# Bucket equality on VectorE instead of sign products on TensorE, for one of eight head groups

## The chip, the cores and the metric

The kernel runs on one core of a Trainium2 chip. The core has a matrix engine (TensorE, PE in the profile; its weight loads are PEld), a vector engine (VectorE, DVE), an activation engine (ScalarE, ACT), a general-purpose one (GpSimd, POOL) and a queue engine (SyncE, SP) that issues most transfers. Each engine takes its instructions in program order and waits on semaphores. The metric is the device time of one execution in microseconds; lower is better.

## The reference

The computation is hash-bucketed attention for 4 batches of 8 heads (sequence 768, head size 64), followed by a channel block with a residual:

```python
q_bits = (np.einsum('bhsd,dk->bhsk', q, proj) > 0)      # 6 bits, k likewise
q_bucket = np.sum(q_bits * powers, axis=-1)             # 0..63
mask = q_bucket[:, :, :, None] == k_bucket[:, :, None, :]
scores = np.where(mask, 0.125 * q @ k.T, -1e9)
attn = softmax(scores) ; x = attn @ v                   # heads side by side: 512 wide
xn = (x - mean) / sqrt(var + 1e-6) * g
out = x + relu(xn @ w_ch1) @ w_ch2                      # 512 -> 2048 -> 512
```

A query sees only keys whose six projection signs are the same as its own.

## The kernel before

**Tiles.** The work is cut into 12 units u (4 batches of 3 query blocks of 256), each unit into 2 head groups g of 4 heads, each group into 3 key pairs kp of 2 x 128 keys. That gives 72 steps, s = 6u + 3g + kp. A step has three parts:

- `S_` (TensorE, line 516): the scores of 4 heads x 256 keys x 256 queries, transposed, into two PSUM tiles (scA, scB). For every 128 keys there are three passes over the 4 heads; each head uses its own 32 rows of the matrix engine, so four matmuls of a pass run side by side. The first pass (`rep == 0`) multiplies the sign rows: `G` holds for every query and key the six signs as +0.5 or -0.5, so the product is 1.5 where all signs agree and at most 1.0 otherwise. The other two passes add q.k, in two halves of 32. q was scaled by 2^-11 before, so that the sign product stands far above it.
- `E_` (ScalarE, line 522): the exponential of 2 heads at a time, with a scale of 256 and a bias that takes the full sign product off again. Where a sign differs, the exponent is lower by 128 or more, and the result is zero. The result is the bf16 tile E, of which there are four buffers.
- `A_` (TensorE, line 541): E as weights times v with a column of ones, 32 matmuls of 65 columns, summed over the three key pairs in one PSUM tile (acc).

After the last key pair of a group, VectorE divides by the sum of the weights (`na`, `nb`), takes statistics (`nc`), and, when both groups are done, centres and scales by g (`ce`). The tile is transposed by a DMA (`fl`). Then `F_` (TensorE, line 598) makes 256 of the 2048 hidden columns at a time, `R_` (relu, line 606 on ScalarE or 608 on VectorE) brings them to SBUF, `D_` (line 614) does a quarter of the second product for one row tile, `Z_` (line 622) adds the residual, `O_` writes the rows out. F has one PSUM bank, so an F waits for the relu of the F before it; D has another.

**Signs.** For batches 1 to 3, `hm` (line 471) multiplies the transposed q and k by the projection into a PSUM tile `hp`: 128 partitions are 4 chunks of the sequence x 4 heads x 8 bit places, 192 columns each for q and k. `bt` (VectorE, line 480) turns it into +-0.5 in bf16, `mw` (line 489) writes that to DRAM and four `mr` (line 492) read it back in the layout that G needs, one head each.

**Order.** Nothing is scheduled at run time. `ORDER` is a list of words such as `S.t.58.2` or `R.v.7.1` (operation, engine, arguments), issued in turn; it fixes the order on every engine's queue and which engine does each relu, copy and cast. `SLOTS` fixes which buffer each tile of a pool takes. In the list, TensorE's score steps, AV steps, F and D alternate, so that ScalarE and VectorE have time between them. The last batch is u = 9, 10, 11 (steps 54 to 71), its second head group the steps 57 to 59, 63 to 65 and 69 to 71.

Of the kernel before, what the change touches and what calls it, by code (L numbers as in the profile page):

```python
# [8 lines left out]
F32 = mybir.dt.float32  # L9
# [5 lines left out]

ROT = (0, 1, 2)
# [3 lines left out]
mem.v lp.a lx.a.0.1.0.1 tab.a pf.v lx.s.0.0.0.1 warm.t wm.t.0 wm.t.1 wm.t.2 wm.t.3 sel.p  # L20
tn.v.0.0.0 p32.p tn.v.0.1.0 ca.p.0.1.0 lx.s.0.1.1.3 ha.t.0.0.0 wm.t.4 lx.s.1.1.0.3 lx.s.1.0.0.1 ha.t.0.1.0 lv.s.0.0.4 ca.a.0.0.0
lx.s.0.0.1.3 bh.v.0.0.0 wm.t.5 tn.v.0.1.1 ha.t.0.1.1 lw2.p.1 bh.v.0.1.0 ca.p.0.1.1 S.t.0.2 lv.s.0.4.4 E.a.0.0 E.a.0.1
tn.v.0.1.2 tn.v.1.1.1 ca.p.1.1.1 lx.s.1.0.1.3 wm.t.6 wm.t.7 bh.v.0.1.1 ha.t.1.1.1 on.p.0 bh.v.1.1.1 tn.v.1.1.0 S.t.1.2
E.a.1.0 ca.v.0.1.2 gx.p.1.0.0 ha.t.0.1.2 bh.v.0.1.2 E.a.1.1 tn.v.1.0.0 ca.p.1.0.0 ca.v.1.1.0 ha.t.1.1.0 bh.v.1.1.0 tn.v.1.1.2
S.t.2.2 E.a.2.0 cv.p.0.0.0 ha.t.1.0.0 bh.v.1.0.0 S.t.4.2 cv.p.0.0.2 tn.v.0.0.1 hc.t.0.0.1 ca.p.0.0.1 lw1.p.3 bc.v.0.0.1
gx.p.1.0.1 ha.t.1.1.2 LX.s.1.0.0 tn.v.0.0.2 E.a.2.1 E.a.4.0 LX.s.1.0.1 E.a.4.1 bh.v.1.1.2 sl.t.0.0.1 bi.v.0.0.1 cv.p.0.4.2
A.t.0.2 S.t.3.2 A.t.1.2 ca.v.1.1.2 lg.s lw1.p.1 sq.t.0.0 E.a.3.0 A.t.2.2 sc.v.0.0 E.a.3.1 S.t.5.2
E.a.5.0 cv.p.0.4.0 sq.t.0.4 na.v.0.0 nb.v.0.0 lw1.p.2 lw1.p.0 nc.v.0.0 E.a.5.1 S.t.8.2 sc.a.0.4 A.t.5.2
E.a.8.0 E.a.8.1 tu.v.1.0.0.2 lw2.p.0 tn.v.1.0.1 A.t.4.2 ca.p.1.0.1 hc.t.0.0.2 tn.v.1.0.2 A.t.3.2 tu.v.1.0.1.0 bc.v.0.0.2
lw2.p.3 gx.p.1.1.1 tu.v.1.0.0.1 sl.t.0.0.2 na.v.0.1 bi.a.0.0.2 S.t.6.2 E.a.6.0 LX.s.1.1.1 E.a.6.1 hc.t.1.0.1 nb.v.0.1  # L30
hc.t.1.0.2 bc.v.1.0.2 sl.t.1.0.2 bi.a.1.0.2 bc.v.1.0.1 pmem.p S.t.7.2 A.t.8.2 E.a.7.0 lv.s.1.4.1 nc.v.0.1 ce.v.0.1
ce.v.0.0 ft.t.0.1 lv.s.1.4.2 E.a.7.1 fc.a.0.1 sl.t.1.0.1 tu.v.1.0.1.1 bi.v.1.0.1 A.t.6.2 ft.t.0.0 S.t.9.2 E.a.9.0
on.p.1 lw2.p.2 fc.v.0.0 E.a.9.1 F.t.0.6 F.t.0.7 tu.v.1.0.1.2 R.a.0.6 A.t.7.2 tu.v.1.0.0.0 S.t.10.2 R.v.0.7
na.v.1.0 nb.v.1.0 lv.s.1.4.0 tu.v.1.0.0.3 tu.v.1.0.1.3 E.a.10.0 CA.p.1.0.1 F.t.0.3 F.t.0.4 E.a.10.1 A.t.9.2 ca.a.0.0.2
R.v.0.4 ca.a.1.0.2 S.t.11.2 gx.p.1.1.0 LX.s.1.1.0 E.a.11.0 E.a.11.1 lv.s.1.0.0 hm.t.1.0 R.v.0.3 F.t.0.5 S.t.14.2
R.a.0.5 A.t.11.2 A.t.10.2 E.a.14.0 E.a.14.1 bt.v.1.0 na.v.1.1 nb.v.1.1 F.t.0.2 R.a.0.2 S.t.12.2 nc.v.1.0
E.a.12.1 E.a.12.0 lv.s.1.0.1 F.t.0.0 R.v.0.0 mw.s.1.0 F.t.0.1 R.a.0.1 CA.p.1.0.0 tu.v.1.1.1.0 A.t.14.2 nc.v.1.1
ce.v.1.0 S.t.13.2 E.a.13.0 D.t.0.0.0 lv.s.1.0.3 tu.v.1.1.1.2 lv.s.1.4.3 D.t.0.0.1 fl.s.1.0 tu.v.1.1.0.2 ce.v.1.1 fl.s.1.1
tu.v.1.1.0.0 A.t.12.2 E.a.13.1 LX.s.2.0.0 S.t.16.2 E.a.16.0 E.a.16.1 A.t.13.2 tu.v.1.1.1.3 tu.v.1.1.0.1 tu.v.1.1.0.3 rs.p.0
D.t.0.0.2 D.t.0.0.3 mr.s.1.0.1 cv.p.1.4.0 Z.v.0.0 tu.v.1.1.1.1 CA.p.1.1.1 cv.p.1.4.2 S.t.15.2 lv.s.1.0.2 cv.p.1.0.0 E.a.15.0  # L40
mr.s.1.0.2 mr.s.1.0.3 hm.t.1.1 E.a.15.1 D.t.0.1.0 CA.a.1.1.0 S.t.17.2 E.a.17.1 mr.s.1.0.0 bt.v.1.1 mw.s.1.1 mr.s.1.1.3
na.v.2.0 nb.v.2.0 F.t.1.2 R.v.1.2 su.p.1.0 A.t.15.2 E.a.17.0 cv.p.1.0.2 A.t.16.2 F.t.1.6 S.t.18.2 R.a.1.6
nc.v.2.0 F.t.1.5 R.v.1.5 D.t.0.1.1 mr.s.1.1.2 E.a.18.0 A.t.17.2 E.a.18.1 sp.t.1.0 sc.v.1.0 na.v.2.1 S.t.20.2
E.a.20.0 mr.s.1.1.0 lv.s.2.4.1 F.t.1.0 tu.v.2.0.0.0 R.v.1.0 D.t.0.1.2 F.t.1.4 nb.v.2.1 nc.v.2.1 E.a.20.1 tu.v.2.0.0.3
R.a.1.4 S.t.19.2 E.a.19.0 E.a.19.1 D.t.0.1.3 ce.v.2.0 F.t.1.1 LX.s.2.0.1 su.p.1.4 rs.p.1 R.a.1.1 mr.s.1.1.1
Z.v.0.1 lv.s.2.0.1 lv.s.2.4.3 O.s.0.1 tu.v.2.0.1.2 lv.s.2.0.2 A.t.20.2 tu.v.2.0.1.1 S.t.21.2 ce.v.2.1 E.a.21.0 fl.s.2.0
F.t.1.3 D.t.1.0.0 E.a.21.1 A.t.18.2 rs.p.2 S.t.22.2 R.v.1.3 tu.v.2.0.0.1 tu.v.2.0.0.2 CA.v.2.0.0 A.t.19.2 fl.s.2.1
F.t.1.7 na.v.3.0 tu.v.2.0.1.3 O.s.0.2 R.v.1.7 E.a.22.0 E.a.22.1 D.t.1.0.1 S.t.23.2 F.t.2.1 lv.s.2.4.0 D.t.1.0.2
R.v.2.1 LX.s.3.1.0 nb.v.3.0 E.a.23.0 A.t.22.2 E.a.23.1 lv.s.2.0.0 F.t.2.0 LX.s.2.1.1 D.t.1.0.3 R.a.2.0 tu.v.2.0.1.0
CA.p.2.0.1 hm.t.2.0 S.t.24.2 E.a.24.1 Z.v.1.0 nc.v.3.0 bt.v.2.0 mw.s.2.0 sp.t.1.4 sc.v.1.4 A.t.21.2 lv.s.2.0.3  # L50
mr.s.2.0.2 D.t.1.1.0 A.t.23.2 O.s.0.0 E.a.24.0 na.v.3.1 O.s.0.3 tu.v.2.1.1.0 F.t.2.3 mr.s.2.0.3 cv.p.2.0.0 tu.v.2.1.1.1
R.a.2.3 nb.v.3.1 S.t.26.2 LX.s.2.1.0 D.t.1.1.1 E.a.26.0 E.a.26.1 nc.v.3.1 F.t.2.2 R.v.2.2 ce.v.3.1 D.t.1.1.2
mr.s.2.0.1 S.t.25.2 ce.v.3.0 F.t.2.4 LX.s.3.0.1 A.t.24.2 E.a.25.0 D.t.1.1.3 cv.p.2.0.2 R.v.2.4 S.t.29.2 E.a.25.1
tu.v.2.1.1.2 fl.s.3.1 Z.v.1.1 E.a.29.0 A.t.25.2 E.a.29.1 D.t.2.0.0 fl.s.3.0 F.t.2.7 R.a.2.7 S.t.28.2 A.t.26.2
tu.v.2.1.0.3 F.t.2.5 D.t.2.0.1 E.a.28.0 R.v.2.5 tu.v.2.1.0.1 E.a.28.1 na.v.4.0 S.t.31.2 E.a.31.1 tu.v.2.1.1.3 F.t.3.6
R.v.3.6 A.t.29.2 D.t.2.0.2 tu.v.2.1.0.2 tu.v.2.1.0.0 CA.v.2.1.0 E.a.31.0 F.t.2.6 R.a.2.6 O.s.1.3 S.t.27.2 E.a.27.0
D.t.2.0.3 nb.v.4.0 LX.s.3.0.0 O.s.1.2 hm.t.2.1 LX.s.3.1.1 nc.v.4.0 bt.v.2.1 mw.s.2.1 mr.s.2.1.3 Z.v.2.0 tu.v.3.0.0.2
E.a.27.1 tu.v.3.0.0.1 S.t.30.2 E.a.30.0 rs.p.3 su.p.2.0 F.t.3.4 A.t.27.2 R.a.3.4 on.p.2 D.t.2.1.0 D.t.2.1.1
E.a.30.1 F.t.3.1 R.v.3.1 S.t.32.2 CA.a.2.1.1 O.s.1.1 E.a.32.0 D.t.2.1.2 lv.s.3.0.0 F.t.3.2 tu.v.3.0.1.0 R.v.3.2
O.s.1.0 A.t.28.2 E.a.32.1 lv.s.2.4.2 S.t.35.2 E.a.35.0 E.a.35.1 na.v.4.1 F.t.3.0 cv.p.2.4.0 mr.s.2.0.0 D.t.2.1.3  # L60
Z.v.2.1 O.s.2.0 A.t.30.2 R.a.3.0 O.s.2.1 S.t.34.2 lv.s.3.0.2 mr.s.2.1.2 F.t.3.3 A.t.31.2 E.a.34.0 nb.v.4.1
R.v.3.3 tu.v.3.0.1.1 nc.v.4.1 ce.v.4.1 D.t.3.0.0 fl.s.4.1 ce.v.4.0 fl.s.4.0 E.a.34.1 tu.v.3.0.1.2 S.t.33.2 rs.p.4
D.t.3.0.1 A.t.32.2 E.a.33.0 tu.v.3.0.0.3 E.a.33.1 F.t.3.5 R.a.3.5 S.t.37.2 E.a.37.1 tu.v.3.0.0.0 cv.p.2.4.2 na.v.5.0
nb.v.5.0 D.t.3.0.2 A.t.33.2 F.t.3.7 A.t.35.2 E.a.37.0 R.v.3.7 nc.v.5.0 S.t.38.2 E.a.38.0 D.t.3.0.3 Z.v.3.0
mr.s.2.1.1 F.t.4.3 A.t.34.2 O.s.2.2 na.v.5.1 E.a.38.1 R.a.4.3 lv.s.3.0.3 O.s.2.3 tu.v.3.0.1.3 S.t.36.2 E.a.36.1
CA.v.3.0.1 F.t.4.0 R.a.4.0 nb.v.5.1 mr.s.2.1.0 CA.v.3.0.0 D.t.3.1.0 hm.t.3.0 bt.v.3.0 E.a.36.0 S.t.39.2 mw.s.3.0
E.a.39.0 F.t.4.2 A.t.38.2 R.a.4.2 tu.v.3.1.1.3 E.a.39.1 A.t.37.2 F.t.4.5 R.a.4.5 S.t.40.2 sp.t.2.0 sc.v.2.0
# [613 lines left out]
```

## Time and profile before

| | |
|---|---|
| runs | 304.79, 305.19 and 303.57 us; median 304.79 |
| profiled execution | 303.7 us; its span 302.0 us, granted TensorE clock 1.0 throughout |
| TensorE busy | 290.5 us (96%) |
| ScalarE busy | 189.0 us (63%) |
| VectorE busy | 175.9 us (58%) |
| GpSimd busy | 76.4 us (25%) |
| 144 exponentials | 153.5 us, 1111 ns each |
| relus | 49 on VectorE (690 ns), 47 on ScalarE (596 ns) |

How to read it: the span is what the profiler saw of one execution, from the first to the last instruction; busy times are unions of an engine's instructions. Matmuls overlap in the matrix engine, so a bar of a matmul is longer than the time that it adds; what a block adds is read from the start of one block to the start of the next. A row of a group gives line, engine, operation, tiles, shapes, count, then busy time and mean duration of one, then the engine's idle time before them and who ended it.

### The profile page before, as it was taken

The page shows a single profiled execution, that of the slowest core. Times are in us where ns is not written, and L with a number is a line of the kernel's source. Part 1 is how long each engine was busy: PE and PEld are TensorE (multiplying, and loading weights), DVE is VectorE, ACT ScalarE, POOL GpSimd, SP SyncE. Part 2 cuts the span into 40 slices and gives each one's busy share as a digit, 9 for nine tenths or more (in the row PEclk, how much of TensorE's full clock was granted, in tenths as well). Part 3 has the DMA queues.
Part 4 walks back from the last instruction along what each step waited for, and adds up shares of the span by engine and source line. Part 5 has one row for each costly group of instructions (what it writes and reads, how often), then busy time and mean ns, then how long its engine had stood idle before and what let it go on. Part 6 is the DMA issues. An engine that isn't in the chain of part 4 may idle for free.

```text
span 302.0 us, 9823 instructions
## 1 busy us (share of the span) xinstructions
PE 290.5 (96%) x4345; PEld 202.5 (67%) x4394; DVE 175.9 (58%) x364; ACT 189.0 (63%) x206; POOL 76.4 (25%) x103
## 2 busy tenths in 40 slices
PE   8988899999999999999999999999999999999995
PEld 4666677676766767677666776667666776676663
DVE  4878758759767564875749466274554346443322
ACT  2587888778646777777667866854565665643010
POOL 5497062476017101300750002700101001001000
PEclk9999999999999999999999999999999999999999
DMA  6999999718768453420322242012201501003132
GB/s 221 310 299 247 282 212 270 177 35 230 201 159 246 84 217 95 98 72 18 80 66 41 68 100 51 21 35 54 54 2 35 106 2 37 20 2 89 52 87 71
DMA packets 31194, 34.32 MB, mean 114 GB/s; under 512 B 15536, under 2 KB 27824, under 8 KB 31152
## 3 DMA queue, kind: packets, MB, share of 16 engines
q1 hardware_dynamic: 26080, 28.98, 35.0%
q0 software_dynamic: 4224, 4.19, 8.5%
q8 instruction: 34, 0.56, 0.8%
q10 hardware_dynamic: 848, 0.53, 0.7%
q14 instruction: 8, 0.07, 0.1%
HBM read 28.12 MB, written 6.88 MB: 116 GB/s over the span
## 4 chain that ended last, share of the span: by engine, by line
PE 94%; ACT 3%; issue 1%; DVE 0%
PE f L598 29%; PE sc L516 19%; PE acc L541 12%; PE hp L471 3%; ACT E L522 3%; PE hf L359 2%; PE warm L328 1%; PE f_110None L614 1%; PE f_101None L614 1%; PE f L614 1%; PE f_90None L614 1%; PE f_20None L614 1%; PE f_80None L614 1%; PE f_21None L614 1%; PE f_00None L614 1%
## 5 line engine op out<-in xcount | busy, mean ns | idle before, releaser
L522 ACT ACTIVATE E<-sc,bias_sb 128x1024 bf16<-128x1024 f32 x144 | 153.5, 1111 | 60.6 <-PE sc L516 60.6
L598 PE MATMUL f<-xnT,w_sb 128*128 128x256 bf16 x768 | 99.3, 273 | 0.1
L598 PEld LDWEIGHTS <-w_sb 128*128 128x128 bf16 x768 | 70.8, 98 | 22.6 <-issue 7.4
L608 DVE TENSOR_SCALAR hb<-f 128x512 bf16<-128x512 f32 x49 | 33.7, 690 | 59.2 <-PE f L598 58.8
L614 PEld LDWEIGHTS <-hb 128*128 128x128 bf16 x400 | 36.0, 98 | 31.2 <-issue 3.0
L516 PE MATMUL sc<-qb,kb 32*128 32x256 bf16 x1152 | 52.4, 267 | 0.0
L606 ACT ACTIVATE hb<-f 128x512 bf16<-128x512 f32 x47 | 28.0, 596 | 35.9 <-PE f L598 35.9
L541 PEld LDWEIGHTS <-E 128*128 128x128 bf16 x1152 | 42.7, 98 | 8.2 <-issue 3.2
L541 PE MATMUL acc<-vaug,E 128*128 128x65 bf16 x1152 | 46.2, 194 | 0.1
L516 PE MATMUL sc<-G 6*128 6x256 bf16 (+1 forms) x576 | 42.6, 273 | 2.7 <-ACT E L522 2.0
L576 POOL TENSOR_SCALAR rs<-mv 128x2 f32<-128x2 f32 x12 | 7.7, 640 | 106.9 <-DVE mv L570 106.6
L516 PEld LDWEIGHTS <-kb 32*128 32x128 bf16 x1152 | 30.4, 93 | 1.5
L516 PEld LDWEIGHTS <-G 6*128 6x128 bf16 (+1 forms) x576 | 15.7, 91 | 20.7 <-issue 17.4
L417 POOL CAST vaug<-vn 128x768 bf16<-128x768 f32 x16 | 14.0, 884 | 58.3 <-DMA vn<-in_v_dram 44.2
L270 DVE STREAM_TRANSPOSE T<-X 128x384 f32<-128x384 f32 (+2 forms) x52 | 26.8, 542 | 1.2 <-DMA X<-in_k_dram 1.2
L554 DVE SCALAR_TENSOR_TENSOR y<-vsB,acc 128x520 f32<-128x520 f32 x24 | 16.5, 688 | 10.5 <-PE acc L541 10.2
L571 DVE SCALAR_TENSOR_TENSOR xc<-x,mv,gB 128x512 bf16<-128x512 f32 x24 | 18.6, 775 | 0.9
L567 DVE BATCH_NORM_STATS2 st<-x 128x6 f32<-128x256 f32 x48 | 17.7, 412 | 0.3
L563 DVE TENSOR_TENSOR x<-y,rc 128x512 f32<-128x512 f32 x24 | 16.8, 699 | 0.8
L425 POOL TENSOR_TENSOR t<-vn 128x768 f32<-128x768 f32 x6 | 10.9, 1812 | 0.0
L281 POOL CAST kb<-T 128x1536 bf16<-128x1536 f32 x3 | 4.4, 1461 | 22.3 <-DVE T L270 22.3
L270 DVE STREAM_TRANSPOSE tp<-X 128x256 f32<-128x256 f32 x24 | 9.0, 416 | 1.4 <-DMA X<-in_q_dram 0.9
(113 smaller groups left out, 236.7 us busy)
## 6 DMA issues: line engine op xcount, KB each, us to landing
out_dram<-x SPq DMA_DIRECT2D x45, 128.0 KB, 2.0
X<-in_k_dram SPq DMA_DIRECT2D x7, 768.0 KB, 5.8
X<-in_q_dram SPq DMA_DIRECT2D x6, 768.0 KB, 4.7
vn<-in_v_dram SPq DMA_DIRECT2D x24, 192.0 KB, 6.0
w_sb<-in_moe_w_ch_dram POOLq DMA_DIRECT2D x8, 512.0 KB, 15.9
vn<-in_v_dram SPq DMA_DIRECT2D x2, 768.0 KB
X<-in_q_dram SPq DMA_DIRECT2D x2, 512.0 KB, 12.2
Bd<-B SPq DMA_DIRECT2D x6, 96.0 KB, 2.5
```

The costliest lines, as they stand in the source:

```text
L270: nc.vector.transpose(d[:, j], s[:, j, kj0 : kj0 + n])
L516: nc.tensor.matmul(sc(s, i // 2)[:, i % 2, 256 * kk : 256 * kk + 256], lh, rh, start=(rep == 0), stop=(rep == 2), skip_group_check=True,)
L522: nc.scalar.activation(E(s)[:, heads(h)], sc(s, h), AF.Exp, scale=EXP_SCALE, bias=bias_sb)
L541: nc.tensor.matmul(acc[:, qt, (D + 1) * i : (D + 1) * (i + 1)], E(s)[:, i, 256 * kk + P * qt : 256 * kk + P * qt + P], vaug(u // 3)[:, 4 * ...
L554: nc.vector.scalar_tensor_tensor(yt(u, g), vs, EPS_ROW, made[f"acc{u}{g}"][:, :, :A], op0=AOP.mult, op1=AOP.add,)
L563: nc.vector.tensor_tensor(xo, a[:, :, :, 0:D], rc.to_broadcast([P, 2, 4, D]), op=AOP.mult)
L567: nc.vector.bn_stats(stats(u)[:, qt, g], xt(u)[:, qt, 256 * g : 256 * g + 256])
L571: nc.vector.scalar_tensor_tensor(xc(u)[:, t], xt(u)[:, t], mv(u)[:, t, 0:1], gB, op0=AOP.subtract, op1=AOP.mult,)
L598: nc.tensor.matmul(f1[:, n].rearrange("p (t x) -> p t x", t=2), w1_sb[:, dt, P * nt : P * nt + P], xnT(u)[:, :, dt], start=(dt == 0), stop ...
L606: nc.scalar.activation(hb(u)[:, 2 * p : 2 * p + 2], f1, AF.Relu)
L608: eng.tensor_scalar_max(hb(u)[:, 2 * p : 2 * p + 2], f1, 0.0)
L614: nc.tensor.matmul(f2, hb(u)[:, nt, P * t : P * t + P], w2_sb[:, nt, half(h)], start=(nt == 0), stop=(nt == NNT - 1),)
```

## The change

For the second head group of the last batch (`COMPARED = ((3, 1),)`) the kernel no longer puts the signs into the scores. Its nine score steps leave the first pass out; the exponential is taken without the bias; and VectorE multiplies the exponentials, in place, by whether the bucket numbers of query and key are equal (`K_`), before A uses them. The bucket numbers are made by seven small matmuls of the +-0.5 signs with powers of two (`nu`): the queries' into 16 partitions, the keys' with the key on the partition, which is how E lies. `ne` copies both out of PSUM; `nw` writes the queries' numbers to DRAM and `nr` reads them back, spread to all 128 partitions (`QB`, 6 KB each), in a buffer of the X pool. The five transfers `mw` and `mr` of this group go. POOL makes the powers of two (`pl`).

`K_` is 4 operations per half step (2 heads x 2 key blocks), 72 in all.

The list ORDER is new as a whole. Up to about u = 4 TensorE's, ScalarE's and VectorE's queues are as before but for single words; behind it F, D, R, A and S stand in another order, 44 relus are on VectorE and 52 on ScalarE, one cast of k or q (`CA.3.1.0`) and two small copies (`sc.3.0`, `sc.3.4`) are on VectorE instead of ScalarE, loads of v stand earlier on SyncE, and at the end part of the last row tile's D stands ahead of the other's.

```diff
+COMPARED = ((3, 1),)
...
+    def pl(eng):
+        nc.gpsimd.memset(zero, 0.0)
+        nc.gpsimd.memset(places, 0.0)
+        for n in range(NB):
+            nc.gpsimd.affine_select(
+                out=places, in_=places, pattern=[[-8, 16]], base=-n, channel_multiplier=1, compare_op=AOP.not_equal, fill=2.0**n,
+            )
...
+    def QB(b, g):
+        return sb(f"QB{b}{g}", [P, 4, S], BF16, "X", 4)
+
+    def nu(eng, b, g):
+        hp = made[f"hp{b}{g}"]
+        nc.tensor.matmul(hp[:16, :W], places, Bt(b, g)[:, 0], start=True, stop=True, skip_group_check=True)
+        kn = hp[:, 384:408].rearrange("p (a k i) -> p a k i", a=2, k=3)
+        for w in range(3):
+            for par in range(2):
+                lo = 64 * ((par + w) % 2)
+                nc.tensor.matmul(
+                    kn[lo : lo + 64, :, (3 * par + w) // 2], Bt(b, g)[:, 1, 64 * w : 64 * w + 64],
+                    places.rearrange("p (a r i) -> p r a i", a=2, r=2)[:, par], start=True, stop=True, skip_group_check=True,
+                )
+
+    def ne(eng, b, g):
+        hp = made[f"hp{b}{g}"]
+        nc.vector.tensor_copy(Qn(b, g), hp[:16, :W])
+        nc.vector.tensor_copy(Kn(b, g).rearrange("p k i -> p (k i)"), hp[:, 384:408])
+
+    def nw(eng, b, g):
+        eng.dma_start(out=Qd(b, g).rearrange("i c w -> c i w"), in_=Qn(b, g))
+
+    def nr(eng, b, g):
+        eng.dma_start(out=QB(b, g).rearrange("p i s -> p (i s)"), in_=Qd(b, g).rearrange("i c w -> (i c w)").partition_broadcast(P))
+
+    def K_(eng, s, h):
+        u, g, kp = s // 6, (s % 6) // 3, s % 3
+        b, q0 = u // 3, 256 * (u % 3)
+        for i in range(4)[heads(h)]:
+            for kk in range(2):
+                e = E(s)[:, i, 256 * kk : 256 * kk + 256]
+                eng.scalar_tensor_tensor(
+                    e, QB(b, g)[:, i, q0 : q0 + 256], Kn(b, g)[:, 2 * kp + kk, i : i + 1], e, op0=AOP.is_equal, op1=AOP.mult,
+                )
...
     def S_(eng, s, h):
...
+            first = 1 if (b, g) in COMPARED else 0
-            for rep in range(3):
+            for rep in range(first, 3):
...
     def E_(eng, s, h):
-        nc.scalar.activation(E(s)[:, heads(h)], sc(s, h), AF.Exp, scale=EXP_SCALE, bias=bias_sb)
+        bias = zero if (s // 18, (s % 6) // 3) in COMPARED else bias_sb
+        nc.scalar.activation(E(s)[:, heads(h)], sc(s, h), AF.Exp, scale=EXP_SCALE, bias=bias)
```

The part of the new list in which the compared steps of u = 9 stand, cut to TensorE's and VectorE's words:

```
S.t.58.2 F.t.6.4 D.t.6.0.0 D.t.6.0.1 R.v.6.4 F.t.7.1 K.v.58.1 R.v.7.1 S.t.57.2 D.t.6.0.2 F.t.7.7 R.v.7.7 A.t.56.2
D.t.6.0.3 Z.v.6.0 K.v.57.0 F.t.7.2 S.t.59.2 D.t.6.1.0 K.v.58.0 F.t.7.0 R.v.7.0 na.v.9.0 D.t.6.1.1 S.t.60.2 F.t.7.3
D.t.6.1.2 D.t.6.1.3 K.v.59.0 F.t.7.5 ce.v.8.0 A.t.58.2 S.t.61.2 K.v.59.1 F.t.7.4 K.v.57.1 A.t.57.2 A.t.59.2 nb.v.9.0
R.v.7.4 F.t.7.6
```

and those around the last ones:

```
S.t.70.2 Z.v.8.1 A.t.66.2 K.v.70.0 K.v.71.0 F.t.10.6 na.v.11.0 D.t.9.0.0 D.t.9.0.1 F.t.10.7 D.t.9.0.2 F.t.10.3 D.t.9.0.3
K.v.69.0 A.t.69.2 F.t.10.1 K.v.70.1 A.t.70.2 nb.v.11.0 Z.v.9.0 A.t.71.2
```

The last D words are, before: `D.11.0.3`, then `D.11.1.0.0 D.11.1.1.0 D.11.1.2.0 D.11.1.3.0` (384 columns) and `D.11.1.0.1` to `D.11.1.3.1` (128 columns); after, `D.11.0.3` is followed only by `D.11.1.3.0` and the last three of 128 columns.

## The prediction

> **What bounds the kernel now.** I read the page's first part, then the windows, then the chain that ended last, and only then the rows of the operations that the change touches.
>
> ```profile
> PE 290.5 (96%) x4345; PEld 202.5 (67%) x4394; DVE 175.9 (58%) x364; ACT 189.0 (63%) x206; POOL 76.4 (25%) x103
> PE 94%; ACT 3%; issue 1%; DVE 0%
> ```
>
> TensorE is busy for 96% of the span and carries 94% of the chain. The windows show where it isn't busy:
>
> ```profile
> 80.00:277.00 197.00, 194.21 (x2927) 135.82 (x2959) 111.74 (x217) 128.39 (x140) 35.24 (x43) 1.00 0.29 74
> 200.00:270.00 70.00, 69.10 (x971) 48.74 (x984) 33.75 (x64) 40.33 (x46) 4.45 (x6) 1.00 0.16 34
> ```
>
> The columns are stretch, length, and busy time of PE, PEld, DVE, ACT, POOL, then the granted clock. In the long middle TensorE misses 2.8 of 197 us, so no new order of the work can win more than that there. From 200 to 270, where S.58 to A.69 of the last batch lie, VectorE works 33.8 of 70 us: 36 us are free, and the change wants most of them.
>
> The chain gives the prices of TensorE's blocks:
>
> ```profile
> 233.28 0.77 PE sc L516 x22
> 234.05 0.98 PE f L598 x8
> 235.03 0.98 PE acc L541 x32
> 236.01 0.87 PE f L598 x8
> ```
>
> A score step S is 0.77 us, and the block behind it is 0.11 longer (0.98 against 0.87), so S counts 0.88. F is 0.87, one AV step A is half of 0.98 = 0.49, a D quarter about 0.87 (1.73 for eight matmuls).
>
> **What the change takes from TensorE.** One score step in detail:
>
> ```profile
> 63.21 0.29 PE L516 MATMUL sc<-G 6*128 6x256 bf16 x4
> 63.33 0.39 PE L516 MATMUL sc<-qb,kb 32*128 32x256 bf16 x8
> 63.55 0.28 PE L516 MATMUL sc<-G 6*128 6x256 bf16 x4
> 63.66 0.39 PE L516 MATMUL sc<-qb,kb 32*128 32x256 bf16 x8
> ```
>
> From the start of a G pass to the next pass are 0.12 and 0.11 us (the bars overlap, since four row groups run together). Nine steps lose both passes: 9 x 0.23 = 2.07 us off the path. Bounds: nothing, if the rest of the step doesn't close up, to a third of 0.88, 9 x 0.29 = 2.6. I take 2.07, the row itself.
>
> **What it adds to TensorE.** nu is one matmul of 192 columns and six of 8 columns. The nearest small ones are the four 64-column matmuls of L383, between 0.11 and 0.21 us start to start (28.37 to 28.58 is the longer). Seven such are 0.2 to 0.37; hm, with 32 matmuls, takes 1.44. I take 0.35. Its wait for bt (0.56 on VectorE) has a score step of 0.77 before it, and F.6.7, which waits for ne (two PSUM copies, about 0.6 us by the 0.56 of bt and the 0.21 of a 64-column one), has D.4.1.3 (0.87) before it. Without those covers it would be 0.5 us.
>
> **What it adds to VectorE.** 72 operations K, scalar_tensor_tensor on 128x256 with two bf16 sources in SBUF and a scalar per partition. No row has just that; the same operation at other lengths is there:
>
> ```profile
> L571 DVE SCALAR_TENSOR_TENSOR xc<-x,mv,gB 128x512 bf16<-128x512 f32 x24 | 18.6, 775 | 0.9
> L622 DVE SCALAR_TENSOR_TENSOR x<-f,rs,x 128x384 f32<-128x384 f32 x1 | 0.6, 618 | 1.8 <-PE f L614 1.8
> L622 DVE SCALAR_TENSOR_TENSOR x<-f,rs,x 128x128 f32<-128x128 f32 x1 | 0.4, 351 | 0.3 <-PE f L614 0.3
> L273 DVE TENSOR_SCALAR G<-hf,hrow 128x256 bf16<-128x256 f32 x2 | 1.0, 484 | 1.4 <-PE hf L359 1.3
> 252.20 0.75 DVE L571 SCALAR_TENSOR_TENSOR xc<-x,mv,gB 128x512 bf16<-128x512 f32 x1
> 252.87 0.20 DVE L570 BATCH_NORM_AGGREGATE mv<-st 128x2 f32<-128x12 f32 x1
> ```
>
> 618 - 351 = 267 ns for 256 elements, 1.04 ns each, so 351 + 133 = 484 ns for 256, which a one-source operation with a scalar per partition indeed takes. Where nothing has to be waited for, the next one starts 0.08 us before the end (0.67 after a start of 0.75). So 0.40 us from K to K, 1.60 for a word of four, 29 us in all. Bounds: 0.484 if each has to end first; below, 351 - 80 = 0.27, if two elements pass per cycle. I take 0.40: both nearest rows say it, and they include bf16 results and SBUF sources.
>
> The Trainium skill (VectorE: DVE Perf Modes, section The perf-mode tier table) has two-tensor operations in 16 bits from SBUF run at two elements per cycle; it lists tensor_tensor and not this operation, and no two-source row here is all 16-bit. By it the price would be an estimated 0.27, and the sum would be that of the first rival below.
>
> **Where the new VectorE work meets the path.** A of these steps now waits for two K words, and relus (R) on VectorE queue behind K; F waits for the R of the F before it, since there is one f1 bank. Over the whole stretch VectorE has room (33.8 + 29 = 63 us, less up to five relus that the new order gives to ScalarE, for 70), so the question is where the order bunches. I add both queues, each to the next start: R 0.61 and Z 0.67 (0.69 and 0.75 less 0.08), na 0.66, ce 0.24 + 0.67 = 0.90, nb 0.24 + 0.71 = 0.95, and the blocks above.
> - *First bunch*, from the start of S.58. TensorE up to A.57: eight F, eight D, three short S (0.65), two S, two A: 6.96 + 6.96 + 1.95 + 1.76 + 0.98 = 18.6. VectorE: K.58.1 can start when the second exp is done, at 0.54 + 0.1 + 1.03 + 1.11 = 2.8; R.7.7 waits for its F until 6.55, Z.6.0 for its D until 7.95. From there it never waits: Z, K.57.0, K.58.0, R, na, K.59.0, ce, K.59.1, K.57.1 = 2.84 + 5 x 1.60 = 10.84, to 18.8, and 0.1 for the signal. A.57 waits 0.3. Then nb.9.0 and R.7.4 end at 20.4, F.7.6 is due at 19.9 and waits 0.5. Sum 0.8; it is nothing at a price of 0.36.
> - *Second bunch.* From S.70, TensorE is at A.69 after 7.2 us (a short S, an A, three F, four D: 0.65 + 0.49 + 2.61 + 3.48). VectorE starts K.70.0 at 1.75 and does K.70.0, K.71.0, na.11.0, K.69.0 by 7.2; A.69 waits 0.1. K.70.1 ends at 8.9 against 8.65: A.70 waits 0.2.
> Together 1.1 us on the path. Each 0.01 us of the price of K moves that by about 0.36 (five words stand in the first bunch, four in the second, four operations each).
>
> **Behind other work.** ScalarE gets five relus (3.0 us) and loses a cast (1.5) and two small copies (0.7): it works 40 of the 70 us. POOL's two memsets and six selects (0.26 each, under 2.2 us) stand ahead of on.2 and cv.2.4, which batch 2's values need much later; su.2.4 and its loads move ahead likewise, and the loads of batch 3's values go ahead of mw.3.0, which went out at 138.0 for an S.54 at 189.4. On SyncE one mw and four mr go and nw and nr come. nr waits on SP for nw to land (2.5 us), and behind it stand O.4.1 and both fl.7, whose xc is written later anyway. nr moves 0.79 MB; loads of X of that size land in 4.7 to 5.8 us, and some 28 us of matmuls (171 to 200) stand between S.50 and S.58. All these at nothing; if the cover failed, K would wait in full. The start of the order, up to about 80 us, is the same queue by queue but for one A.
>
> **The end.** In the profile the last TensorE work is at 298.3, the last result leaves at 298.7 and the span ends at 302.0.
>
> ```profile
> 295.64 3.55 ACTq L634 DMA_DIRECT2D out_dram<-x  x3
> 294.85 0.75 DVE L622 SCALAR_TENSOR_TENSOR x<-f_110None,rs,x 128x512 f32<-128x512 f32 x1 [1.09 <-PE f_110None L614]
> 297.40 0.62 DVE L622 SCALAR_TENSOR_TENSOR x<-f,rs,x 128x384 f32<-128x384 f32 x1 [1.79 <-PE f L614]
> 298.29 0.35 DVE L622 SCALAR_TENSOR_TENSOR x<-f,rs,x 128x128 f32<-128x128 f32 x1 [0.28 <-PE f L614]
> ```
>
> Now 3.5 us of matmuls stand between D.11.0.3 and the end; the new order leaves 1.3, having put half of the other row tile's D earlier. Z.11.0 and its 0.26 MB of output thus come 2.2 us closer to the end, and three pairs of issues (0.54 each) follow one another. The last issue is 0.7 instead of 0.4 us behind TensorE: +0.36. The two outputs (0.52 MB) then go out in one piece; the first took 1.1 us and the second 1.2, so that the last byte could be 0.87 later. I take +0.6.
>
> **Sum**: -2.07 + 0.35 + 1.1 + 0.6 = 0.0. The profiled execution took 303.7 us (span 302.0 and 1.7 around it), 1.1 under the median of the runs shown (304.79, from 303.57 to 305.19); I put the difference on the median: 304.8 us. Differences under 0.5%, 1.5 us, count as none, about what the spread of these runs can tell.
>
> **Rivals.**
> 1. *VectorE keeps up.* At 0.27 per K neither bunch forms: -2.07 + 0.35 + 0.6 = -1.1, 303.7 us. For it: both sources are 16-bit, and the plain scaling of 1536 f32 in SBUF (0.96 us) does run at two per cycle. Against: the two-source rows don't.
> 2. *VectorE becomes the bound of the last batch.* It decides from 0.44 per K, where the two bunches cost 2.6 us; at 0.45 they cost 2.9, net +1.8, 306.6 us; at the full 0.484, 4.1, net +3.0, 307.8. For it: in the first bunch VectorE has no pause for 11 us, so whatever is added to K goes straight on. Against: independent operations overlap by 0.08 in every row.
> 3. *The change doesn't do what it says on TensorE*: the weight loads of the step hold it, and 16 matmuls last as long as 24: +2.1, 306.9 us. Against: each pass has its own 0.11 in the timeline.
> 4. *The spread bucket numbers come late* and K.58.1 waits for nr: it would need a landing over 20 us; +5, 310.
>
> **Chances.** Forecast 0.45, rivals 0.20, 0.27, 0.05, 0.03. Faster by over 0.5% needs rival 1 with no loss at the end (-1.7): 0.08 of its 0.20, and 0.07 from the rest by the spread of the runs, 0.15. Slower by over 0.5%: rivals 2 to 4 and a little of the forecast, 0.36. The forecast's own range is 304.0 to 305.9. The range reaches from rival 1 with half its end loss, less 0.3 for the spread, to rival 2 near its upper end: 303.2 to 307.4.
>
> **What would show it.** S steps of the last group at 0.54 (0.77 if rival 3); K at 484 ns and 0.40 start to start (351 and 0.27 if rival 1); waits of A.57, F.7.6, A.69 and A.70 on VectorE, 1.1 us in all; the end of TensorE 1 us earlier or less, and 0.4 to 0.9 us more from there to the end of the span. Wrong would make it above all a K price beyond 0.37 to 0.43.

## The result and the profile after

The changed kernel takes 306.12 us (median of 9 runs, 305.54 to 307.0); the kernel before took 304.53 beside it (9 runs, 303.57 to 305.19). The ratio is 1.0054, with a 95% interval from 1.0036 to 1.0072: 1.6 us slower, just past the 0.5% at which a difference was to count. The forecast was 304.8, no change. The profiled execution took 306.8 us, its span 305.1.

The first part of the page of the changed kernel and the engines of its chain:

```profile
PE 289.8 (95%) x4282; PEld 201.7 (66%) x4329; DVE 201.5 (66%) x436; ACT 189.7 (62%) x208; POOL 77.4 (25%) x111
PE 78%; DVE 8%; DMA 5%; POOL 3%; issue 3%; SPq 1%; ACT 1%; DVEq 0%
```

TensorE has 0.7 us less to do, VectorE 25.6 more, and VectorE, which was on 0% of the chain, is on 8%: waits on it now lie on the path. The same two windows as before (stretch, length, busy time of PE, PEld, DVE, ACT, POOL, granted clock, share of DMA, GB/s):

```profile
80.00:277.00 197.00, 193.38 (x2877) 134.72 (x2913) 138.68 (x292) 129.40 (x141) 35.61 (x51) 1.00 0.30 78
200.00:270.00 70.00, 68.39 (x856) 46.38 (x865) 55.41 (x124) 42.51 (x49) 3.99 (x6) 1.00 0.18 41
```

From 200 to 270 VectorE works 55.4 of 70 us instead of 33.8 (the forecast was under 63), and TensorE misses 1.6 us instead of 0.9. Of the 1.6 only 0.67 is a wait, the one shown below; the rest, and all of the 0.9, are gaps of about 0.2 us at blocks of which the trace has one matmul too few. The second profile of the kernel before, taken for another reason below, has no such gap: 70.00 of 70 there, and 197.00 of 197 in the longer window. VectorE has 14.6 us left there, so on the average of the stretch it isn't the bound. The new operations have these rows:

```profile
L552 DVE SCALAR_TENSOR_TENSOR E<-QB,Kn,E 128x256 bf16<-128x256 bf16 x72 | 29.5, 478 | 2.5 <-ACT E L583 2.5
L530 PE MATMUL hp<-places,B 128*64 128x8 bf16 x6 | 0.3, 180 | 0.0
L525 PE MATMUL hp<-B,places 128*16 128x192 bf16 x1 | 0.3, 251 | 0.0
```

K takes 478 ns (484 was the estimate). Where the path meets it, TensorE's timeline of the last batch reads (start, length, operation; in brackets the idle time ahead and what ended it):

```profile
219.46 1.05 PE L659 MATMUL f<-xnT,w_sb 128*128 128x256 bf16 x8
220.34 1.15 PE L602 MATMUL acc<-vaug,E 128*128 128x65 bf16 x32
222.16 1.03 PE L659 MATMUL f<-xnT,w_sb 128*128 128x256 bf16 x8 [0.67 <-DVE hb L669]
223.13 0.62 PE L576 MATMUL sc<-qb,kb 32*128 32x256 bf16 x16
223.67 1.04 PE L675 MATMUL f_70None<-w_sb,hb 128*128 128x512 bf16 x3
```

The score step is short as intended: 0.54 us from 223.13 to the next block, 0.77 in the other groups. The F ahead of it, F.7.6, waits 0.67 us for a relu. VectorE's timeline says why that relu is late:

```profile
216.75 0.75 DVE L632 SCALAR_TENSOR_TENSOR xc<-x,mv,gB 128x512 bf16<-128x512 f32 x1
217.42 3.25 DVE L552 SCALAR_TENSOR_TENSOR E<-QB,Kn,E 128x256 bf16<-128x256 bf16 x8
220.59 0.20 DVE L622 RECIPROCAL rc<-y 128x8 f32<-128x8 f32 x1
220.82 0.69 DVE L624 TENSOR_TENSOR x<-y,rc 128x512 f32<-128x512 f32 x1
221.43 0.68 DVE L669 TENSOR_SCALAR hb<-f 128x512 bf16<-128x512 f32 x1
```

F.7.4 is done at about 220.5. Its relu stands behind eight K and nb, and starts at 221.43. In the chain of waits two K words, eight operations, count for 3.16 us, 0.395 from start to start; the first bunch is there, as long as forecast.

A second wait was not foreseen. It is for the transposed tile, in TensorE's and SyncE's timelines:

```profile
275.91 3.17 SPq L641 DMA_TRANSPOSE xnT<-xc  x2
280.50 1.03 PE L659 MATMUL f<-xnT,w_sb 128*128 128x256 bf16 x8 [0.43 <-DMA xnT<-xc]
```

The two issues of the transposition take 3.17 us on SyncE, and F.11.2 waits 0.43. Before, the same two took 2.50 and nothing waited for them. The account of the prediction comes back to this wait.

The end of the changed kernel, in the timeline without TensorE:

```profile
298.71 0.75 DVE L683 SCALAR_TENSOR_TENSOR x<-f_110None,rs,x 128x512 f32<-128x512 f32 x1 [1.32 <-PE f_110None L675]
299.38 0.95 DVE L683 SCALAR_TENSOR_TENSOR x<-f,rs,x 128x384 f32<-128x384 f32 x2
299.49 2.12 SPq L695 DMA_DIRECT2D out_dram<-x  x3
299.49 1.83 ACTq L695 DMA_DIRECT2D out_dram<-x  x3
```

Z.11.0 starts at 298.71, 1.2 us ahead of the last matmul's end (299.94); before it was 3.4 ahead. All six issues follow in one run. From the last matmul to the end of the span are 5.15 us instead of 3.74.

### The profile page after: what moved, and what is told of

Read it like the earlier page. It is cut to its first block, busy times and chain, and to the rows that moved or that the text cites. A ratio compares the mean times of both kernels' runs of the same rounds, so it can differ in the third digit from the quotient of the medians.

```text
span 305.1 us, 9775 instructions
## 1 busy us (share of the span) xinstructions
PE 289.8 (95%) x4282; PEld 201.7 (66%) x4329; DVE 201.5 (66%) x436; ACT 189.7 (62%) x208; POOL 77.4 (25%) x111
## 4 chain that ended last, share of the span: by engine, by line
PE 78%; DVE 8%; DMA 5%; POOL 3%; issue 3%; SPq 1%; ACT 1%; DVEq 0%
PE f L659 25%; PE sc L576 14%; PE acc L602 9%; DVE E L552 3%; DMA X<-in_k_dram 3%; PE hp L474 2%; PE hf L362 2%; DMA G<-Bd 1%; DVE T L273 1%; PE warm L331 1%; PE f_101None L675 1%; PE f_91None L675 1%; PE f_51None L675 1%; PE f_21None L675 1%; PE f_20None L675 1%
## 5 line engine op out<-in xcount | busy, mean ns | idle before, releaser
L583 ACT ACTIVATE E<-sc,bias_sb 128x1024 bf16<-128x1024 f32 x126 | 134.1, 1111 | 51.7 <-PE sc L576 50.6
L667 ACT ACTIVATE hb<-f 128x512 bf16<-128x512 f32 x52 | 31.0, 596 | 42.0 <-PE f L659 42.0
L669 DVE TENSOR_SCALAR hb<-f 128x512 bf16<-128x512 f32 x44 | 30.2, 689 | 39.9 <-PE f L659 39.3
L576 PE MATMUL sc<-qb,kb 32*128 32x256 bf16 x1152 | 51.5, 268 | 0.0
L602 PEld LDWEIGHTS <-E 128*128 128x128 bf16 x1152 | 42.2, 98 | 6.5 <-issue 2.9
L602 PE MATMUL acc<-vaug,E 128*128 128x65 bf16 x1152 | 45.3, 194 | 0.1
L576 PE MATMUL sc<-G 6*128 6x256 bf16 (+1 forms) x504 | 37.6, 273 | 2.7 <-ACT E L583 2.0
L576 PEld LDWEIGHTS <-kb 32*128 32x128 bf16 x1152 | 29.7, 93 | 3.3 <-issue 1.9
L552 DVE SCALAR_TENSOR_TENSOR E<-QB,Kn,E 128x256 bf16<-128x256 bf16 x72 | 29.5, 478 | 2.5 <-ACT E L583 2.5
L576 PEld LDWEIGHTS <-G 6*128 6x128 bf16 (+1 forms) x504 | 13.9, 91 | 18.8 <-issue 15.6
L583 ACT ACTIVATE E<-sc,zero 128x1024 bf16<-128x1024 f32 x18 | 19.4, 1110 | 7.0 <-PE sc L576 6.9
```

Of the source, the lines that this page charges most:

```text
L552: eng.scalar_tensor_tensor(e, QB(b, g)[:, i, q0 : q0 + 256], Kn(b, g)[:, 2 * kp + kk, i : i + 1], e, op0=AOP.is_equal, op1=AOP.mult,)
L576: nc.tensor.matmul(sc(s, i // 2)[:, i % 2, 256 * kk : 256 * kk + 256], lh, rh, start=(rep == first), stop=(rep == 2), skip_group_check=True,)
L583: nc.scalar.activation(E(s)[:, heads(h)], sc(s, h), AF.Exp, scale=EXP_SCALE, bias=bias)
L602: nc.tensor.matmul(acc[:, qt, (D + 1) * i : (D + 1) * (i + 1)], E(s)[:, i, 256 * kk + P * qt : 256 * kk + P * qt + P], vaug(u // 3)[:, 4 * ...
L667: nc.scalar.activation(hb(u)[:, 2 * p : 2 * p + 2], f1, AF.Relu)
L669: eng.tensor_scalar_max(hb(u)[:, 2 * p : 2 * p + 2], f1, 0.0)
```

## The experiments

Each was timed in five rounds beside the kernel before on the same chip, but for one that was only profiled. Two ratios of separate comparisons differ by chance by up to some 0.0025, 0.8 us.

**The end alone.** The last words of ORDER as in the kernel before, the rest as changed.

```diff
-D.t.11.1.0.0 O.s.10.1 F.t.11.3 D.t.11.0.0 ... D.t.11.1.1.0 D.t.11.1.2.0 O.s.8.3 F.t.11.6 R.v.11.6 D.t.11.1.0.1 ... D.t.11.0.3 Z.v.11.0
+F.t.11.3 D.t.11.0.0 ... F.t.11.6 R.v.11.6 ... D.t.11.0.3 D.t.11.1.0.0 D.t.11.1.1.0 D.t.11.1.2.0 D.t.11.1.3.0 Z.v.11.0
```

> The changed kernel with the last row tile's D words put back behind D.11.0.3, as before the change; nothing else moved. Theory (the loss sits in the new order, not in the exchange of sign products for equality): from the last matmul to the end of the span falls from 5.1 us to about 3.7, and the time falls by 1.0 to 1.4 us, from 306.1 to about 305.0. Rival (the end is late because of the transfers of that one execution): no change within 0.4 us.

305.33 us against 304.41, ratio 1.0033 (1.0014 to 1.0052). From the last matmul to the end of its span are 4.13 us instead of 5.15. The new end costs about 0.7 us of time, which alone is within what two comparisons can differ by; in these two traces it is 1.0. The twelve profiles of this case agree on it: the five with the new end have 5.0 to 5.3 us behind the last matmul, the seven with the old end 3.7 to 4.3.

**The start alone.** A of step 3 back where it was, between hc and sl of the same tile.

```diff
-tn.v.1.0.1 A.t.3.2 sc.a.0.4 ... E.a.8.1 on.p.1 hc.t.0.0.2
+tn.v.1.0.1 sc.a.0.4 ... E.a.8.1 on.p.1 hc.t.0.0.2 A.t.3.2
```

> The changed kernel with one AV step, A.3, put back behind hc.0.0.2, where it covers VectorE's Bc. Theory: the 0.58 us wait of sl.0.0.2 for Bc near 29 us goes, and the time falls by 0.5 us, to 305.6. Rival (the start is late by its loads and by the clock of that execution): the wait goes and comes back elsewhere in the start, no change.

306.10 us, ratio 1.0051 (1.0025 to 1.0077): no gain that can be measured. Its profile can't decide why. sl still waits 0.78 us there, but in that execution a load of k landed late (the transposition that waits for it started at 29.1, against 27.2 to 28.7 in the others), and the copy that sl waits for stands behind it on VectorE. The second profile of the kernel before, below, comes back to this place.

**Without the comparisons.** The changed kernel without its 72 K words.

```diff
-K.v.58.1 K.v.57.0 K.v.58.0 K.v.59.0 K.v.59.1 K.v.57.1 ... K.v.69.0 K.v.70.1
```

> The changed kernel without the 72 equality products on VectorE (the equality of buckets is left out in the second head group of the last batch). Theory: the waits of F.7.6 for its relu (0.67 us) and of F.11.2 for its transposed tile (0.43) go, nothing else: 1.1 us, to 305.0. Rival (VectorE is the bound of the last batch): 2 to 4 us less, under 304.

304.89 us, ratio 1.0017 (0.9998 to 1.0036), so the comparisons cost 1.2 us of 306.12 at that place of the order. The wait at F.7.6 is gone, that at F.11.2 is 0.27, and VectorE works 28.6 us from 200 to 270:

```profile
200.00:270.00 70.00, 70.00 (x901) 47.67 (x900) 28.62 (x54) 41.95 (x48) 4.43 (x6) 1.00 0.17 41
```

**The order without the exchange.** The changed kernel's order, but with the sign passes in all groups, no nu, ne, pl and K, and mw and four mr where nw and nr stand.

```diff
-COMPARED = ((3, 1),)
+COMPARED = ()
-nu.t.3.1 ... ne.v.3.1 ... nw.s.3.1 ... nr.s.3.1
+mw.s.3.1 ... mr.s.3.1.0 mr.s.3.1.1 mr.s.3.1.2 mr.s.3.1.3
```

> The new order with the change undone: signs in the scores everywhere, the five transfers of signs back, no bucket numbers and no equality products. Theory: the new order costs 2 us by itself: 2.0 for the sign passes come back, 0.55 for the bucket matmuls and 1.1 for VectorE's waits go, so 306.4, and 2 us above the kernel before. Rival (the order is neutral and the exchange costs 1.6 us): 304.5, as before.

305.94 us, ratio 1.0049 (1.0033 to 1.0065): 1.5 us slower than the kernel before with the same arithmetic. The new order costs all of the loss. The exchange itself, put on top of it, moves the time by 0.2 us, less than can be told from nothing. By the profiles most of the 1.5 us is the end: here 5.0 us follow the last matmul, where the two profiles of the kernel before have 3.7 and 3.8. From the first score step to the last matmul TensorE takes 289.7 us, against 289.1 and 289.4, and 0.35 of that is a wait at the start, which the second profile of the kernel before, below, explains.

**The exchange in the old order.** Start and end of the kernel before; nu and ne between S of step 50 and two covering blocks; K one to three blocks behind their exponentials, with many relus, F, D and A between step 55 and the D of unit 10 moved to make room.

```diff
-bt.v.3.1 ... S.t.50.2 E.a.50.1 su.p.3.0 F.t.5.0 R.v.5.0 A.t.46.2 D.t.4.1.3
+bt.v.3.1 ... S.t.50.2 E.a.50.1 su.p.3.0 nu.t.3.1 ne.v.3.1 A.t.46.2 D.t.4.1.3 ... F.t.5.0 R.v.5.0
```

> The exchange in the order of the kernel before: its first 80 us, its end from the last reads of f2 on and its blocks stay as they were, except that nu goes between S of step 50 and two blocks that cover its copies, the K stand one to three blocks behind their exponentials, and relus and third blocks around steps 55 to 71 are shifted so that none has to queue behind a K. Theory (the exchange is a gain of 2.0 us, less about 0.55 for nu, and VectorE's 28.5 us cost only where they stand in a relu's or an A's way; the rest of the change's loss is its new order): 302.9 to 303.6 us where the kernel before has 304.4, a ratio of 0.995 to 0.997, with no wait over 0.3 us at F of units 7 to 11. Rival (VectorE's load cannot be hidden at this density, whatever the order): 304.3 us or more, with waits for hb or E of over 1.2 us in all.

304.50 us against 304.69, ratio 0.9987 (0.9971 to 1.0003). No wait of F is over 0.3 us, as the theory had it, but the time is a microsecond above it.

**The shorter steps alone.** The kernel before with the sign passes of the compared group left out.

```diff
+            first = 1 if (b, g) == (3, 1) else 0
-            for rep in range(3):
+            for rep in range(first, 3):
```

> The kernel before, word for word, but that the nine steps of the compared group leave the sign passes out and nothing takes their place (the bucket equality of that group is left out; its sign rows are still loaded). Theory (each of the nine steps is 0.22 to 0.23 us shorter on the path and nothing else ends there): 2.0 us off, 302.4 us, ratio 0.9934. Rival (the shorter steps are given back because the exponentials, the relus or the transposed tiles are then late): 303.4 us or more, with new waits of over 1 us on TensorE behind step 57.

302.83 us, ratio 0.9940 (0.9919 to 0.9961): 1.9 us off. From the start of the last hm to the last matmul's end are 126.6 us (296.5 - 170.0), against 128.4 in the kernel before (298.7 - 170.3, second profile). Eight of the nine steps are 0.22 us shorter to the next block. S.65, which stands between two F, is only 0.02 shorter (0.75 after 0.77), for there the second F waits for the relu of the first. So 1.8 us is what the exchange has to pay from.

**One relu on ScalarE.** The changed kernel with the relu of F.7.4 taken out of VectorE's bunch.

```diff
-E.a.61.0 K.v.59.1 fl.s.8.1 F.t.7.4 K.v.57.1 A.t.57.2 E.a.61.1 A.t.59.2 nb.v.9.0 R.v.7.4 F.t.7.6
+E.a.61.0 K.v.59.1 fl.s.8.1 F.t.7.4 R.a.7.4 K.v.57.1 A.t.57.2 E.a.61.1 A.t.59.2 nb.v.9.0 F.t.7.6
```

> The changed kernel with one relu, that of F.7.4, on ScalarE, ahead of the second exponential of step 61, instead of on VectorE behind the comparisons of steps 59 and 57. Theory (the 0.67 us that F.7.6 waits are that relu's place in VectorE's queue): the wait is gone and the time falls by 0.3 to 0.7 us, to 305.5 us or so against 304.4 before, ratio 1.0035. Rival (the lost time only moves on, to the exponential that now stands behind the relu, or to the next A behind a K): no wait at F.7.6, but as much at S of step 64 or A of 60 to 62, and 306.1 us, ratio 1.0055.

305.39 us against 304.69, ratio 1.0023 (1.0010 to 1.0037). TensorE's timeline at that place:

```profile
219.50 1.15 PE L602 MATMUL acc<-vaug,E 128*128 128x65 bf16 x32
220.48 1.04 PE L659 MATMUL f<-xnT,w_sb 128*128 128x256 bf16 x8
221.45 0.61 PE L576 MATMUL sc<-qb,kb 32*128 32x256 bf16 x16
```

F.7.6 starts 0.98 after the two A and waits for nothing. The 0.7 us stayed gained.

**The kernel before once more**, for a second profile of its start.

> The kernel before once more, for a second profile. Theory (the start's 0.6 us to TensorE's full clock and the pause ahead of sl near 29 us vary from execution to execution): TensorE reaches its full clock at another moment than 5.8 us, by up to 1.3 us, and a pause of 0.3 us or more ahead of sl appears. Rival (the new order makes that pause): none before sl.

Its rows there, and those of the changed kernel (both timelines; L541 and L602 are A, L370 and L373 hc, L383 and L386 sl):

```profile
26.42 1.15 PE L541 MATMUL acc<-vaug,E 128*128 128x65 bf16 x32
27.50 0.43 PE L370 MATMUL hf<-tp,p 128*32 128x64 f32 x16
27.86 0.66 PE L541 MATMUL acc<-vaug,E 128*128 128x65 bf16 x16
28.36 0.28 PE L383 MATMUL hf<-Bc,spread 128*128 128x64 bf16 x4
```

```profile
26.87 1.64 PE L602 MATMUL acc<-vaug,E 128*128 128x65 bf16 x48
28.45 0.43 PE L373 MATMUL hf<-tp,p 128*32 128x64 f32 x16
28.72 0.58 DVE L273 STREAM_TRANSPOSE T<-X 128x384 f32<-128x384 f32 x1 [1.72 <-DMA X<-in_k_dram]
29.46 0.28 PE L386 MATMUL hf<-Bc,spread 128*128 128x64 bf16 x4 [0.58 <-DVE Bc L276]
```

The rival is right: in the kernel before an A stands between hc and sl and hides VectorE's copy of hc's result; sl starts 0.50 after that A, its usual length. In the changed order all three A stand ahead of hc, and sl waits for the copy. A late load of k, for which VectorE waits just ahead of that copy, can make sl wait in either order. With A behind hc sl waits for nothing in five of seven profiles, and 0.34 and 0.78 in two with a late load; with A ahead of hc it waits 0.35 to 0.58 in all five. TensorE's full speed came at 6.1 us instead of 5.8, a little of what the theory said of the start.

**Four places mended.** The changed kernel with the old end, A of step 3 back, the relu of F.7.4 on ScalarE, and F.11.2 one block later.

```diff
-D.t.10.0.1 F.t.11.2 R.a.11.2 D.t.10.0.2 F.t.11.0 R.a.11.0 D.t.10.0.3 Z.v.10.0 F.t.11.1 R.v.11.1 D.t.10.1.0
+D.t.10.0.1 D.t.10.0.2 F.t.11.2 R.a.11.2 D.t.10.0.3 Z.v.10.0 F.t.11.0 R.a.11.0 D.t.10.1.0 F.t.11.1 R.v.11.1
```

> The changed kernel with four places of its order mended at once: the last D words as before, A of step 3 back between hc and sl, the relu of F.7.4 on ScalarE, and F.11.2 one D block later, with the D of unit 10 moved up one place. Theory (these waits are the price of the new order and add up: 0.8 for the end, 0 to 0.35 for the start, 0.7 for the relu, 0.3 to 0.6 for the transposed tile): 303.7 to 304.3 us where the kernel before has 304.6 and the changed one 306.1, ratio 0.997 to 0.999. Rival (a wait that goes from one place comes back at the next, and VectorE's comparisons keep their 1.2 us): 305 us or more, ratio above 1.0013.

303.68 us against 304.43, ratio 0.9974 (0.9958 to 0.9989): 2.4 us better than the changed kernel, and 0.75 better than the one before. The four prices (0.7, up to 0.35, 0.7, 0.43) add up to 2.2. Its stretch, the place of F.11.2, and its end:

```profile
200.00:270.00 70.00, 69.11 (x887) 47.47 (x897) 55.66 (x125) 42.96 (x50) 3.99 (x6) 1.00 0.17 41
```

```profile
279.32 1.04 PE L662 MATMUL f<-xnT,w_sb 128*128 128x256 bf16 x8
280.19 1.03 PE L678 MATMUL f_100None<-w_sb,hb 128*128 128x512 bf16 x4
...
294.85 0.75 DVE L686 SCALAR_TENSOR_TENSOR x<-f_110None,rs,x 128x512 f32<-128x512 f32 x1 [1.19 <-PE f_110None L678]
295.63 3.54 SPq L698 DMA_DIRECT2D out_dram<-x  x3
```

VectorE has the same 55.7 us to do, and TensorE misses 0.9 of 70 again, as in the kernel before, with no wait among it. F.11.2 (279.32) no longer waits, and Z.11.0 with its outputs is back 3.4 us ahead of the last matmul's end (298.2). The mended order wasn't run without the exchange, so how much of the 0.75 us is the exchange's and how much the order's isn't shown.

**The exchange in the old order without the comparisons.** It splits what the exchange in the old order has lost against the shorter steps alone.

```diff
-K.v.58.1 K.v.58.0 K.v.59.1 K.v.57.0 K.v.59.0 K.v.57.1 ... K.v.70.0 K.v.70.1
```

> The exchange in the order of the kernel before, word for word, but that the 72 K are left out (the bucket equality of the compared group is left out; its numbers are still made, spread and loaded). It splits the 1.7 us that lie between the exchange in the old order and the shorter steps alone. Theory (nu and its moved blocks cost 0.55 us and the comparisons about 1.1, though no single wait over 0.15 us shows): 303.4 us where the kernel before has 304.7, ratio 0.9957. Rival (the comparisons are hidden there, and the moved blocks and nu cost all of it): 304.3 us or more, ratio 0.9985.

304.57 us against 304.43, ratio 1.0005 (0.9989 to 1.0022). The rival is right: without the 28.5 us of comparisons it isn't faster than with them (0.9987). In that order they are hidden, and nu with the moved blocks costs all: from the last hm to the last matmul's end are 128.1 us without K and 127.9 with them, against 126.6 for the shorter steps alone. nu itself has 0.37 of it, from its start to the A behind it, in the old order with the exchange:

```profile
172.65 0.25 PE L528 MATMUL hp<-B,places 128*16 128x192 bf16 x1
172.83 0.26 PE L533 MATMUL hp<-places,B 128*64 128x8 bf16 x6
173.02 0.66 PE L605 MATMUL acc<-vaug,E 128*128 128x65 bf16 x16
```

The rest comes in pieces of 0.1 to 0.2 us, wherever one block stands alone between two F. Here is a short step behind a D (S.57 in the shorter steps alone), then one between two F (S.59 in the old order with the exchange):

```profile
204.74 1.03 PE L615 MATMUL f_60None<-w_sb,hb 128*128 128x512 bf16 x4
205.70 0.62 PE L517 MATMUL sc<-qb,kb 32*128 32x256 bf16 x16
206.25 1.05 PE L599 MATMUL f<-xnT,w_sb 128*128 128x256 bf16 x8
```

```profile
209.30 1.03 PE L662 MATMUL f<-xnT,w_sb 128*128 128x256 bf16 x8
210.26 0.61 PE L579 MATMUL sc<-qb,kb 32*128 32x256 bf16 x16
211.02 1.03 PE L662 MATMUL f<-xnT,w_sb 128*128 128x256 bf16 x8
```

Behind a D the short step passes in 0.55 us. Between two F it is the only cover of a relu, and the second F starts 0.76 after it: the time that the step gave up comes back as a wait. An ordinary step or a D alone between two F takes 0.08 us longer than elsewhere where the relu is on VectorE (0.69), and no longer where it is on ScalarE (0.60). Behind the last hm the old order with the exchange has eleven such places, two of them short steps, and loses 1.1 us at them; the shorter steps alone have two and lose 0.3. With nu's 0.37 that is 1.2 of the 1.4 us between the two. The blocks that I moved made these places.

## Why the prediction was wrong by 1.3 us

The forecast was 304.8 us and no change; it became 306.1, at the edge between no change and slower. That lies in the stated range (303.2 to 307.4), but above the forecast's own (304.0 to 305.9). It is partly luck: the upper part of the range stood for rival 2, a higher price of K, and K cost what was forecast. What was missed are terms that the sum put at nothing or too low. Step by step:

- *The shorter steps (-2.07).* The mechanism is right: 1.8 us in the traces, 1.9 in time, 0.54 or 0.55 to the next block. The 0.2 that are missing are S.65, which stands between two F.
- *nu (+0.35).* Right: 0.37 from its start to the next block in the old order. TensorE is 0.5 us later by the end of unit 5 there; most of the rest is S.49, alone between two F (0.85 instead of 0.77).
- *The price of K (0.40 from start to start).* Right: 478 ns, 0.395 apart, where two elements per cycle would have left 0.27. The first rival falls with that. The Trainium skill (VectorE: DVE Perf Modes, section The perf-mode tier table) gives tensor_tensor two elements per cycle with 16-bit sources in SBUF, and has no row for this operation. The trace has 478 ns with both sources in bf16 and SBUF, so that rule does not extend to it.
- *The first bunch (+0.8).* The mechanism is right and shown by two runs: F.7.6 waits 0.67 (0.5 forecast) for a relu behind K, and one relu on ScalarE takes 0.7 us off. A.57 does not wait (0.3 forecast).
- *The second bunch (+0.3).* The wrong wait: A.69 and A.70 wait for nothing. What waits is F.11.2, for the transposed tile, and that is the slow issue's doing. In the changed kernel and the runs with the old end, the old start and the moved relu the two issues took 3.17, 3.63, 3.37 and 3.29 us, and F.11.2 waited 0.43, 0.88, 0.62 and 0.59: always what goes beyond 2.70 to 2.75. At the usual 2.50, which the order without the exchange has, nothing waits. Without K the issues took 3.29 and F.11.2 waited 0.27, so K uses up some 0.3 us of the room there, and no more. That 1.1 us of waits agree with the 1.2 by the run without K is thus in part chance.
- *"All these at nothing", the start.* This step failed. "The same queue by queue but for one A" was true; that this A was the cover of the copy ahead of sl I had not looked up. By the traces it costs 0.35 us or more; the run with A alone put back could not resolve that in the time.
- *The end (+0.6).* The mechanism is right, the size was not. Between the medians of the profiles with either end lie 1.1 us, and the run with the old end shows 0.7 in time. I had added the delay of the last issue and half of the bytes. The last issue is done 1.67 us behind the last matmul instead of 1.20, 0.47 for the 0.36 forecast; the other 0.6 come behind it, and why isn't settled.

What the sum has too little is thus the end (0.1 by the time, 0.5 by the traces), the start (0.35) and the shorter steps (0.2): 0.65 to 1.05 of the 1.6 us. The rest isn't settled, and is no more than two comparisons can differ by. Single executions differ by as much: 0.43 us go to a wait of sp for a sum on POOL at 68 us in the profile of the changed kernel, 0.37 in that of the mended order and 0.27 in the second of the kernel before, and 0.12 or nothing in the others.

The second rival, VectorE as the bound, does not hold either: where K stand in the old order, the same work on VectorE costs less than can be measured, and in the mended order TensorE waits for nothing between 200 and 270. What the change loses, it loses by its order: 1.5 us with no exchange at all.

## What to carry to other kernels

When a change comes with a new order of the work, run the new order without the change: here the order took 1.5 us and the exchange itself nothing that could be measured, and four small repairs turned 0.5% slower into 0.26% faster. Two of the four, the relu and F.11.2, mend waits that only the exchange brings. Work moved to an idle engine costs only where something on the path queues behind it, so look for the relu, copy or transposition behind each bunch rather than at the engine's share. And a block that is moved or shortened may have been a cover: for each, name the result that is made while it runs, and who waits for that.

## What the runs showed of the hardware

TensorE starts at half speed, and when it comes to full speed differs from execution to execution. The warm-up matmuls are 128x512; here are the first four of wm (line 331 before, 334 and 335 after the change) in the kernel before, in the changed kernel, and in the one without comparisons:

```profile
4.50 1.68 PE L331 MATMUL warm<-ones 128*128 128x512 bf16 x4
```

```profile
4.50 1.92 PE L334 MATMUL warm<-ones 128*128 128x512 bf16 x4
```

```profile
4.35 1.03 PE L335 MATMUL warm<-ones 128*128 128x512 bf16 x4
```

Four at full speed take 1.03 us, four at half speed 1.92. The granted clock reads 1.00 in all three. By the pace of the matmuls, the change to full speed lies between 4.2 and 7.1 us after the start over the twelve profiles of this case, and the first score step starts between 8.4 and 9.8 us. Two profiles of one kernel differ in it too (5.8 and 6.1 in the kernel before), so a profile's start can be off another's without any cause in the kernel: the changed kernel's profile, at 7.0, had 0.6 us of this.

The other surprise is SyncE: of the last two issues of a transposition, the first took 1.86 us in the changed kernel and 1.89 in the mended one, where 1.2 is usual. In both the queue had issued nothing for 10 us before, but that isn't the cause: in the changed kernel two other transpositions came after 13 us without an issue and took 1.2, and one right behind another issue took 2.13. This last pair is long (3.2 to 3.6 us) in all eight profiles with the exchange's transfers (nw, nr) and 2.50 in all four with mw and mr; why isn't settled.
